# Sharing VectorE's shift passes with GpSimd, DMA transposes and a new fill rule in an interleaved attention kernel

## The chip, the cores and the metric

The kernel runs on one core of a Trainium2 chip. The metric is the device time of one execution in microseconds (us), lower is better. Each quoted time is the median of several executions of one kernel. A profile is one such execution, read by the hardware profiler.

## The reference, cut to what matters

Four blocks in a row work on 2048 rows of 512 numbers: attention block A, linear attention block B, then A and B again with the same weights. Nearly all of the time is in A: 32 heads share one key and value head of width 16, and each head needs a full 2048 x 2048 table of exponentials.

```python
def _A_ref(x, wq, wk, wv, wo):
    H = 32; Dh = D // H                          # D = 512, Dh = 16
    q = (x @ wq).reshape(B, S, H, Dh)            # S = 2048 (transposed to heads first)
    k = x @ wk                                   # one key head for all 32
    v = x @ wv
    scores = jnp.einsum("bhqd,bkd->bhqk", q, k) * (Dh ** -0.5)
    p = _softmax(scores, axis=-1)
    return jnp.einsum("bhqk,bkd->bhqd", p, v)... @ wo
# _B_ref: phi(t) = where(t > 0, t + 1, exp(t)) + 1e-6 of q and k, then linear attention
x = x + _A_ref(_layernorm(x), ...);  x = x + _B_ref(_layernorm(x), ...)
x = x + _A_ref(_layernorm(x), ...);  x = x + _B_ref(_layernorm(x), ...)
```

## The kernel before: the parts that matter

The program has no hand-written order. It describes operations with an estimated duration for each, and a small list scheduler runs them on a model clock while the program is being built. The engine of each operation and the order on each engine are then fixed, and semaphores hold the dependencies. An estimate in the program decides the order, but it is not a time on the chip.

The scores of the two A blocks fall into 2 x 2048 = 4096 tiles of 128 x 512. Each goes one of two ways:

- **ScalarE's way.** TensorE writes two or three score tiles into PSUM, ScalarE takes their exponential, and TensorE multiplies the result by the values (one pass per tile).
- **VectorE's way.** VectorE builds the bits of a bfloat16 exponential with integer arithmetic. A first pass reads the scores from PSUM. Three *shift passes* then add 32, 64 and 96 to the 16-bit words of four tiles at once, from SBUF to SBUF, and TensorE sums the four terms with weighted values (four value passes per tile).

```python
# one first pass per tile (PSUM -> SBUF)
o = add(DV, tdv(512), lambda e: e.tensor_scalar(out=PTD[:, hp.idx, 0, i * 512:(i + 1) * 512], in0=bank(db),
        scalar1=SCALE * LOG2E * 128.0, scalar2=TOFF, op0=ALU.mult, op1=ALU.add), ..., name="P1")
# after four of them: three shift passes per group, all on VectorE (SBUF -> SBUF)
for r in range(NTERM):                           # NTERM = 4
    dep = c["p1"]
    if r:
        dep = [add(DV, tdv(512 * m, 0.26), lambda e, r=r: e.tensor_scalar(out=PTD[:, hp.idx, r, 0:512 * m],
                   in0=PTD[:, hp.idx, 0, 0:512 * m], scalar1=float(SHIFT[r]), scalar2=None, op0=ALU.add),
                   deps=c["p1"], uses=[hp], prio=3.0, name="xo")]
    for i, p in enumerate(c["pos"]):
        pv = self.add_pv(p, PTD[:, hp.idx, r, i * 512:(i + 1) * 512].bitcast(BF16), hp, dep[0 if r else i], r, 1)
# ... cut: buffer release ...
# phi of block B: the exponential on ScalarE, then on GpSimd
o2 = add(PO, 0.65, lambda e: e.tensor_scalar(out=e_buf[:, he.idx, :], in0=e_buf[:, he.idx, :],
        scalar1=1.0, scalar2=1e-6, op0=ALU.min, op1=ALU.add), ..., name="phm")
# ... cut: VectorE combines max(scores, 0) with it; layer norm, transposes on TensorE, projections, ramp, tail
```

`DV` is VectorE, `PO` is GpSimd, `AC` is ScalarE. `idle()` (cut) adds filler matmuls where the model expects TensorE to be idle for long; they are meant to keep its granted clock up.

The softmax here doesn't subtract the row's maximum and nothing guards it: scores larger than these inputs give would overflow.

Of the kernel before, what the change touches and what calls it, by code (L numbers as in the profile page):

```python
# [14 lines left out]
LAT = {PE: 0.2, AC: 0.22, DV: 0.13, PO: 0.2, SP: 2.0}  # L15
STATS = {}
FLEX = 0.0
SWITCH, PASS = 0.1, 0.217
MP, AP, MF, AF = 1, 2.0, 0.4, 2.0

# [27 lines left out]
class Sched:  # L48
# [152 lines left out]
    def _start(self, e, o):  # L201
# [19 lines left out]
        o.vis = end + (3.0 if o.dma else LAT[e])  # L221
# [39 lines left out]
    def finalize(self):  # L261
# [20 lines left out]
        for e in self.engs:  # L282
            n = 0
            for o in self.order[e]:
                if o.dma:
                    o.val = 16
                elif o.marked:
                    n += 1
                    o.val = n
            STATS["sem_" + e] = n  # L290
# [6 lines left out]
    def emit(self, name, eng):  # L297
        for o in self.order[name]:
            best = {}
            for d in o.waits:  # L300
                key = ("dma", id(d)) if d.dma else d.eng
                if best.get(key, (None, -1))[1] < d.val:
                    best[key] = (d, d.val)
            for d, v in best.values():
                eng.wait_ge(self.dsems[id(d)] if d.dma else self.sems[d.eng], v)
            ins = o.fn(eng)
            if o.dma:
                ins.then_inc(self.dsems[id(o)], 16)
            elif o.marked:
                ins.then_inc(self.sems[name], 1)  # L310


class Banks:
# [7 lines left out]
    def slots(self, idx, kind):  # L321
        if kind == "set":
            return (3 * idx, 3 * idx + 1, 3 * idx + 2)
        if kind == "set2":
            return (3 * idx, 3 * idx + 1)
# [30 lines left out]
def bass_interleave_layers__grouped_kv_mqa__linear_attn_block__prompt_kernel(  # L356
# [17 lines left out]
    LEAD = 16  # L374
    KC = 2
    HOLD = 0.75
    PCONT = 1.5
    DB = (5, 6)
# [3 lines left out]
    AWIN, ATGT, ATGT2 = 1.7, 0.5, 0.6  # L382
# [32 lines left out]
    NPA, NPD = 5, 3  # L415
    PTA = sb("PTA", [P, NPA, 1536], BF16)
    PTD = sb("PTD", [P, NPD, NTERM, 2048], U16)
# [47 lines left out]
    def dma(fn, **kw):  # L465
        return add(SP, 0.08, fn, dma=True, **kw)

# [43 lines left out]
    def layer_norm(t, prio, cb, win=None):  # L511
# [5 lines left out]
        else:  # L517
            add(DV, 0.062, lambda e: e.tensor_scalar(out=veps[:, t:t + 1], in0=mv[:, t, 1:2], scalar1=1e-5, scalar2=None, op0=ALU.add),  # L518
                reads=[("mv", t)], writes=[("ve", t)], prio=prio - 0.02)
            add(PO, 0.5, lambda e: e.tensor_tensor(out=rstd[:, t:t + 1], in0=veps[:, t:t + 1], in1=mhalf[:, 0:1], op=ALU.pow),  # L520
                reads=[("ve", t), "mhalf"], writes=[("rs", t)], prio=prio)
        hx, hb = Holder(p_xn), H_()
        o = add(DV, tdv(512, 0.52), lambda e: e.tensor_scalar(out=xn_buf[:, hx.idx, :], in0=x_sb[:, t, :], scalar1=mv[:, t, 0:1],
                                                              scalar2=rstd[:, t:t + 1], op0=ALU.subtract, op1=ALU.mult),
                reads=[("x", t), ("mv", t), ("rs", t)], prio=prio - 0.03, acq=[hx], name="xn")

# [10 lines left out]
        o2 = add((DV, AC), {DV: 0.333, AC: tac(512)}, cp, deps=[o], uses=[hb], rel=[hb] + ([win] if win else []), writes=[("xnT", t)], prio=prio - 0.04, name="xnT", cb=cb)  # L537
# [51 lines left out]
    def q_proj(L, qb, g, prio):  # L589
# [7 lines left out]
        o2 = add((DV, AC), {DV: tdv(512), AC: tac(512)}, ev, deps=[o], uses=[h], rel=[h], writes=[("QT", qb % 2, g, t) for t in range(4)], prio=prio - 0.05, name="qev")  # L597
# [3 lines left out]
    def q_tile(L, t, prio):  # L601
# [14 lines left out]
        o2 = add((DV, AC), {DV: tdv(512), AC: tac(512)}, ev, deps=[o], uses=[h], rel=[h], writes=[("QT", 0, g, t) for g in range(NG)], prio=prio - 0.05, name="qev")  # L616
# [4 lines left out]
    class Ctl:  # L621
        def __init__(self):
# [4 lines left out]
            self.pd = 0  # L627
            self.taken = bytearray()
# [5 lines left out]
            self.tail = True  # L634

# [62 lines left out]
        def add_pv(self, p, src, hold, dep, r=0, wt=NTERM):  # L698
# [25 lines left out]
            def f(e):  # L724
                return e.matmul(ps[32 * c:32 * c + 32, 7 * 512:8 * 512], lhsT=Vaug[:, kt, r, :], rhs=src, start=opened[0], stop=opened[1],  # L725
# [36 lines left out]
        def step(self, now):  # L762
# [9 lines left out]
            if self.pa >= n:  # L772
                self.tail = True
                for b in DB:
                    self.dstep(b, set())
                return False
            for s in ((0,) if self.ramp else (0, 1)):
                if not (banks.free[3 * s] and banks.free[3 * s + 1]):
                    continue
                w = 3 - s  # L780
                if w == 3 and not banks.free[3 * s + 2]:
                    continue
# [11 lines left out]
                if HOLD < 3.0 and not self.ramp and not any(banks.free[b] for b in DB) and self.dcan():  # L794
# [4 lines left out]
                kind = "set" if w == 3 else "set2"  # L799
# [8 lines left out]
            if not self.ramp and sum(not o.done for o in self.p1s) < DMIN:  # L808
# [8 lines left out]
        def fill(self, s, got, kind):  # L817
# [15 lines left out]
            def f(e):  # L833
                if twice:
                    self.smm(e, got, 3 * s)
                return self.smm(e, got, 3 * s)
# [7 lines left out]
            oe = add(AC, tac(m * 512), lambda e: e.activation(PTA[:, hp.idx, 0:m * 512], bank(3 * s, m * 512), ACTF.Exp, scale=SCALE),  # L844
# [13 lines left out]
        def dstep(self, db, js):  # L858
# [6 lines left out]
            if not banks.free[db] or (db == 6 and self.waiting()):  # L865
                return False
            if self.dcur is None:
                if not p_ptd.free:
                    return False
                hp = Holder(p_ptd)  # L870
# [11 lines left out]
            if p >= n or not self.ok(p):  # L882
# [11 lines left out]
            o = add(DV, tdv(512), lambda e: e.tensor_scalar(out=PTD[:, hp.idx, 0, i * 512:(i + 1) * 512], in0=bank(db), scalar1=SCALE * LOG2E * 128.0,  # L894
# [9 lines left out]
        def dpass(self, c):  # L904
            hp = c["hp"]
            m = len(c["pos"])
            cnt = {"n": 0}
            for r in range(NTERM):
                dep = c["p1"]
                if r:  # L910
                    dep = [add(DV, tdv(512 * m, 0.26), lambda e, r=r: e.tensor_scalar(out=PTD[:, hp.idx, r, 0:512 * m], in0=PTD[:, hp.idx, 0, 0:512 * m], scalar1=float(SHIFT[r]),  # L911
                                                                                   scalar2=None, op0=ALU.add),
                               deps=c["p1"], uses=[hp], prio=3.0, name="xo")]
                for i, p in enumerate(c["pos"]):
                    pv = self.add_pv(p, PTD[:, hp.idx, r, i * 512:(i + 1) * 512].bitcast(BF16), hp, dep[0 if r else i], r, 1)
                    cb0 = pv.cb

                    def cb(o_, cb0=cb0):
                        cb0(o_)
                        cnt["n"] += 1  # L920
                        if cnt["n"] == m * NTERM:
                            sc.at(o_.vis, lambda: p_ptd.give(hp.idx, None))
                    pv.cb = cb

        def dcan(self):
            return not self.dhold() and (self.dcur is not None or bool(p_ptd.free))

        def dhold(self):
            return self.pa + LEAD + 4 >= len(self.pos)
# [3 lines left out]

    def activity(now):

        tot, first = 0.0, now
        for o in reversed(sc.order[PE]):
# [3 lines left out]
            if o.pk[0] == "P":  # L941
                b = min(b, first)
                first = min(first, o.t0)
            if b > a:
                tot += (b - a) * (RG / P * len(o.pk[1]) if o.pk[0] == "S" else 0.95)
        return tot / AWIN

    def idle(now):
# [20 lines left out]
        else:  # L969
            c = max(range(4), key=lambda c: sc.pgrp.get(c, 0.0) if sc.pk == "P" else 0.0)  # L970
            f = lambda e: e.matmul(ps[32 * c:32 * c + 32, 7 * 512:8 * 512], lhsT=zer[:, 0:32], rhs=maskx[:].bitcast(BF16)[:, 0:512],  # L971
                                   start=not owned, stop=True, skip_group_check=True)
            pk = ("P", (c,))
# [8 lines left out]
    def for_misc():  # L982
        if ctl.tail or (ctl.ramp and not (ctl.layer is not None and ctl.ok(0))):
            return (6, 5, 4, 3, 2, 1, 0)
        return (6, 5, 4, 3) if ctl.ramp else (6,)
# [4 lines left out]
    def epi_tr(L, qb, g, hos, fine):  # L990
        h = H_()
        pr = 4.0
        keys = [("OT", gg, g) for gg in range(NG)] if fine else [("OT", g, qs) for qs in range(4)]

# [10 lines left out]
        o2 = add((DV, AC), {DV: 0.333, AC: tac(512)}, cp, deps=[o], uses=[h], rel=[h], writes=keys, prio=pr, name="otc")  # L1005
# [6 lines left out]
    def epi_y(L, qb, qs):  # L1012
# [4 lines left out]
            deps=[o], uses=[h], rel=[h], writes=[("x", t)], prio=2.0, name="res", cb=lambda o_: b_prep(L, t))  # L1017


    def phi(h, o, dst, keys, prio, tiled=False):  # L1020
        he = Holder(p_e)
        o1 = add(AC, tac(512), lambda e: e.activation(e_buf[:, he.idx, :], bank(h.idx), ACTF.Exp), deps=[o], uses=[h], acq=[he], prio=0.5, name="phe")  # L1022
        o2 = add(PO, 0.65, lambda e: e.tensor_scalar(out=e_buf[:, he.idx, :], in0=e_buf[:, he.idx, :], scalar1=1.0, scalar2=1e-6, op0=ALU.min, op1=ALU.add),  # L1023
                 deps=[o1], uses=[he], prio=prio, name="phm")
        sh = (lambda a: a.rearrange("p (g n) -> p g n", g=NG)) if tiled else (lambda a: a)
        add(DV, tdv(512), lambda e: e.scalar_tensor_tensor(out=dst, in0=sh(bank(h.idx)), scalar=0.0, in1=sh(e_buf[:, he.idx, :]), op0=ALU.max, op1=ALU.add),  # L1026
            deps=[o2], uses=[h, he], rel=[h, he], writes=keys, prio=prio - 0.1, name="phf")

    def b_prep(L, t):
        def go(o_):  # L1030
# [11 lines left out]
            o2 = add((DV, AC), {DV: tdv(512), AC: tac(512)}, ev, deps=[o], uses=[h2], rel=[h2], writes=[("vB", t % NTK)], prio=2.1, name="vBe")  # L1042
# [5 lines left out]
            elif t % 4 == 3:  # L1048
                b = t // 4
                for g in range(NG):  # L1050
                    h = H_()
                    o = proj(h, [(wqkv_sb[:, ft, g * P:(g + 1) * P], xnT[:, ft, b * 512:(b + 1) * 512]) for ft in range(FT)], 512,
                             ["wqkv"] + [("xnT", tt) for tt in range(4 * b, 4 * b + 4)], pr + 0.2, name="pq")
                    phi(h, o, pqT[:, g, b * 512:(b + 1) * 512], [("pq", g, tt) for tt in range(4 * b, 4 * b + 4)], 2.4)
            if t == T - 1:
                b_main(L)
        layer_norm(t, 2.3, go)

# [13 lines left out]
    def kv_block(L, b):  # L1072
        tl = KVB[b]
        n, final = len(tl), b == len(KVB) - 1
        for hh in range(2):
            h = H_()
            o = None
            for i, t in enumerate(tl):
# [9 lines left out]
                o = add(PE, 0.172, f, reads=[(k, tt % NTK) for k in ("pk", "vB") for tt in rd], prio=3.4, name="kv", pk=ALL4, **kw)  # L1088
            dst = kvacc if b == 0 else kvtmp
            add(DV, tdv(KW), lambda e, hh=hh, h=h, dst=dst: e.tensor_tensor(out=dst[:, hh, :], in0=bank(h.idx, KW), in1=maskx[:], op=ALU.mult),  # L1090
                reads=["mask"], deps=[o], uses=[h], rel=[h], writes=[("kva" if b == 0 else "kvt", hh)], prio=1.9, name="kvm")
# [116 lines left out]
```

## Time and profile before

| | before |
|---|---|
| time at the outset, median of 3 | 1684.43 us (1681.29 to 1697.97) |
| ScalarE busy, all / score exponentials | 1530.4 / 1430.7 us |
| score tiles: ScalarE / VectorE | 3099 / 997 |
| VectorE busy | 1415.1 us (84%) |
| GpSimd busy | 170.5 us (10%) |
| mean granted TensorE clock | 0.973 |

The groups by shape of the kernel before. The columns are: line, engine, operation, output <- input, shapes, count | busy us, mean ns of one | idle us before, and what ended it. L844 is ScalarE's exponential, L894 VectorE's first pass, L911 its shift pass, L1023 GpSimd's min-then-add.

```profile
L844 ACT ACTIVATE PTA<-ps_all 128x1536 bf16<-128x1536 f32 x632 | 933.1, 1476 | 72.6 <-PE ps_all L688 68.9
...
L894 DVE TENSOR_SCALAR PTD<-ps_all 128x512 uint16<-128x512 f32 x997 | 676.3, 684 | 153.4 <-PE ps_all L688 149.0
L844 ACT ACTIVATE PTA<-ps_all 128x1024 bf16<-128x1024 f32 x601 | 632.6, 1053 | 17.1 <-PE ps_all L688 16.3
...
L911 DVE TENSOR_SCALAR PTD<-PTD 128x2048 uint16<-128x2048 uint16 x744 | 496.4, 685 | 5.0
...
L1023 POOL TENSOR_SCALAR e_buf<-e_buf 128x512 f32<-128x512 f32 x64 | 126.6, 1978 | 701.7 <-ACT e_buf L1022 686.0 <-ACT veps L515 7.8 <-ACT rstd L516 7.4
```

One ScalarE tile costs 1430.7 / 3099 = 0.46 us. A first pass or a shift pass takes about 685 ns as recorded; in the timeline consecutive ones start 0.60 us apart. Shift passes fill 499 us of VectorE.

Two of the table of 25 us windows (stretch, length, busy us of each engine with its instruction count, granted TensorE clock, DMA share, GB/s). In the first ScalarE is busy almost throughout, which is the rule in the steady stretches; in the second the clock has fallen and everything has slowed.

```profile
core 0: us, PE busy (x) PEld busy (x) DVE busy (x) ACT busy (x) POOL busy (x), PEclk, DMA share, GB/s
100.00:125.00 25.00, 23.84 (x233) 7.24 (x225) 22.03 (x41) 23.61 (x22) 3.25 (x2) 1.00 0.01 2
1000.00:1025.00 25.00, 24.34 (x151) 5.08 (x145) 15.18 (x26) 17.62 (x15) 0.00 (x0) 0.58 0.00 1
```

From the list of waits (who <- for whom: us in total, times, longest us):

```profile
DVE PTD L894 <- PE ps_all L688: 149.0, 248, 3.2
...
ACT PTA L844 <- PE ps_all L688: 85.3, 108, 7.4
...
DVE pqT L1026 <- POOL e_buf L1023: 35.5, 22, 6.5
DVE pk_tok L1026 <- POOL e_buf L1023: 25.4, 28, 1.5
```

ScalarE loses 85 us to late score matmuls. Last, a detail: a shift pass on VectorE that begins just after a GpSimd operation. These are the timelines of VectorE and of GpSimd (start us, us, engine, line, operation).

```profile
721.00 1.11 DVE L911 TENSOR_SCALAR PTD<-PTD 128x2048 uint16<-128x2048 uint16 x1
722.03 0.68 DVE L894 TENSOR_SCALAR PTD<-ps_all 128x512 uint16<-128x512 f32 x1
```
```profile
720.96 1.92 POOL L1023 TENSOR_SCALAR e_buf<-e_buf 128x512 f32<-128x512 f32 x1 [10.73 <-ACT e_buf L1022]
```

The shift pass started 0.04 us after GpSimd's min-then-add and took 1.11 us in place of 0.69, but it ended 0.77 us before GpSimd did.

### The profile page before, as it was taken

Reading aid. Unit: us, or ns where it says so; the run is one execution under the profiler, and the core shown is the slowest. Engines: PE = TensorE matmul, PEld = TensorE weight load, DVE = VectorE, ACT = ScalarE, POOL = GpSimd, SP = SyncE. Lnnn points to the kernel's source line nnn. Section 1 sums busy time; section 2 is a strip of 40 time slices with the busy share of each in tenths; the row PEclk is TensorE's granted clock in tenths of the full one; section 3 lists DMA queues with packets and bytes.
Section 4 is the critical chain, followed back from the end, with each engine's and each line's share of the span. In section 5 each row is a group of like instructions: output and inputs, shape, how many; then the busy total and the mean of one; then the engine's idle time right before and its main releaser. Section 6 shows DMA issues by size and latency. Waiting matters only on the chain.

```text
span 1694.3 us, 40968 instructions
## 1 busy us (share of the span) xinstructions
PE 1602.4 (95%) x18333; PEld 531.1 (31%) x18333; DVE 1415.1 (84%) x2525; ACT 1530.4 (90%) x1496; POOL 170.5 (10%) x157
## 2 busy tenths in 40 slices
PE   7999999999999799999899999999999999899998
PEld 4323223323333133332543222223332332232334
DVE  6898898889898588987788887788998888788875
ACT  6999999999999599998699988899999999899866
POOL 2000000010010101012210000001000100001032
PEclk9999999999999799999999988899999999999999
DMA  3000000000000000000000000000000000000001
GB/s 127 1 2 1 2 1 1 2 1 1 2 1 2 0 2 1 1 2 2 3 3 1 1 1 1 1 1 2 2 1 1 1 2 1 1 1 1 1 2 52
DMA packets 7776, 9.99 MB, mean 6 GB/s; under 512 B 1456, under 2 KB 7088, under 8 KB 7600
## 3 DMA queue, kind: packets, MB, share of 16 engines
q1 hardware_dynamic: 7600, 7.37, 1.3%
q8 instruction: 143, 2.34, 0.6%
q14 instruction: 33, 0.27, 0.1%
HBM read 5.28 MB, written 2.10 MB: 4 GB/s over the span
## 4 chain that ended last, share of the span: by engine, by line
PE 45%; ACT 34%; DVE 13%; POOL 6%; issue 2%; DMA 0%; SPq 0%; POOLq 0%; ACTq 0%
ACT PTA L844 32%; PE ps_all L688 18%; PE ps_all L725 17%; PE ps_all L459 6%; POOL e_buf L1023 6%; DVE PTD L894 4%; DVE PTD L911 3%; PE ps_all L746 2%; ACT e_buf L1022 1%; DVE pk_tok L1026 1%; DVE pqT L1026 1%; DVE Eo L737 1%; DVE stats L512 1%; PE ps_all L971 1%; PE ps_all L530 1%
## 5 line engine op out<-in xcount | busy, mean ns | idle before, releaser
L844 ACT ACTIVATE PTA<-ps_all 128x1536 bf16<-128x1536 f32 (+1 forms) x1234 | 1430.7, 1269 | 89.7 <-PE ps_all L688 85.3
L894 DVE TENSOR_SCALAR PTD<-ps_all 128x512 uint16<-128x512 f32 x997 | 676.3, 684 | 153.4 <-PE ps_all L688 149.0
L688 PE MATMUL ps_all<-QT,Kr 32*128 32x512 bf16 x4201 | 721.5, 388 | 21.7 <-DVE PTD L894 10.3
L725 PE MATMUL ps_all<-PTD,Vaug 128*32 128x512 bf16 x3988 | 586.4, 392 | 9.7 <-DVE Eo L737 7.6
L725 PE MATMUL ps_all<-PTA,Vaug 128*32 128x512 bf16 x3099 | 553.8, 393 | 0.5 <-ACT PTA L844 0.3
L911 DVE TENSOR_SCALAR PTD<-PTD 128x2048 uint16<-128x2048 uint16 (+1 forms) x750 | 499.3, 684 | 5.0
L688 PEld LDWEIGHTS ps_all<-QT,Kr 32*128 32x128 bf16 x4201 | 177.2, 91 | 528.0 <-ACT PTA L844 208.3
L725 PEld LDWEIGHTS ps_all<-PTD,Vaug 128*32 128x32 bf16 x3988 | 143.5, 95 | 198.8 <-issue 128.2
L725 PEld LDWEIGHTS ps_all<-PTA,Vaug 128*32 128x32 bf16 x3099 | 132.2, 94 | 208.6 <-issue 182.5
L1023 POOL TENSOR_SCALAR e_buf<-e_buf 128x512 f32<-128x512 f32 x64 | 126.6, 1978 | 701.7 <-ACT e_buf L1022 686.0
L520 POOL TENSOR_TENSOR rstd<-veps,mhalf 128x1 f32<-128x1 f32 x26 | 23.2, 894 | 739.6 <-DVE veps L518 685.8
L459 PE MATMUL ps_all<-wqkv_sb,xnT 128*32 128x512 bf16 x1024 | 81.6, 386 | 8.5 <-DVE pk_tok L1026 7.1
L1022 ACT ACTIVATE e_buf<-ps_all 128x512 f32<-128x512 f32 x64 | 39.2, 612 | 19.7 <-PE ps_all L459 19.3
L746 PE MATMUL ps_all<-identf,Eo 128*128 128x128 f32 x256 | 44.7, 300 | 11.9 <-DVE pk_tok L1026 8.4
L459 PE MATMUL ps_all<-xnT,wqkv_sb 128*32 128x128 bf16 (+1 forms) x896 | 41.3, 300 | 11.7 <-DVE pqT L1026 10.9
L1026 DVE SCALAR_TENSOR_TENSOR pqT<-ps_all,e_buf 128x512 bf16<-128x512 f32 x32 | 21.9, 689 | 35.6 <-POOL e_buf L1023 35.5
L459 PE MATMUL ps_all<-xnT,wq_sb 128*32 128x128 bf16 (+1 forms) x896 | 44.8, 301 | 3.5 <-issue 3.4
L512 DVE BATCH_NORM_STATS2 stats<-x_sb 128x6 f32<-128x512 bf16 x64 | 42.8, 676 | 2.8 <-DMA x_sb<-in_A_x_dram 2.7
L737 DVE COPY Eo<-ps_all 128x512 f32<-128x512 f32 x63 | 42.9, 681 | 1.9 <-PE ps_all L746 1.2
L1026 DVE SCALAR_TENSOR_TENSOR pk_tok<-ps_all,e_buf 128x512 bf16<-128x512 f32 x32 | 22.1, 691 | 25.5 <-POOL e_buf L1023 25.4
L459 PE MATMUL ps_all<-wo_sb,OT 128*32 128x512 bf16 x512 | 41.2, 382 | 0.3 <-DVE pqT L1026 0.2
L746 PEld LDWEIGHTS ps_all<-identf,Eo 128*128 128x128 f32 x256 | 28.6, 148 | 32.2 <-DVE pk_tok L1026 12.7
(82 smaller groups left out, 707.8 us busy)
## 6 DMA issues: line engine op xcount, KB each, us to landing
out_dram<-x_sb SPq DMA_DIRECT2D x16, 128.0 KB, 1.7
x_sb<-in_A_x_dram SPq DMA_DIRECT2D x3, 512.0 KB, 6.7
wqkv_sb<-in_B_wqkv_dram SPq DMA_DIRECT2D x1, 1536.0 KB, 12.1
x_sb<-in_A_x_dram SPq DMA_DIRECT2D x2, 256.0 KB, 3.1
wq_sb<-in_A_wq_dram SPq DMA_DIRECT2D x1, 512.0 KB, 4.9
wo_sb<-in_A_wo_dram SPq DMA_DIRECT2D x1, 512.0 KB, 8.5
wo_sb<-in_B_wo_dram SPq DMA_DIRECT2D x1, 512.0 KB, 11.5
wk_sb<-in_A_wk_dram SPq DMA_DIRECT2D x1, 16.0 KB, 2.5
```

The lines of the kernel that those rows point to most:

```text
L459: i = e.matmul(out[32 * c:32 * c + 32], lhsT=lhsT[:, 32 * c:32 * c + 32], rhs=rhs, start=start, stop=stop, skip_group_check=True)
L512: add(DV, tdv(512), lambda e: e.bn_stats(stats[:, t, 0:6], x_sb[:, t, :]), reads=[("x", t)], writes=[("st", t)], prio=prio, name="bn")
L688: x = e.matmul(bank(b0 + k), lhsT=Kr[r, m, kt * P:(kt + 1) * P], rhs=QT[r, self.units[u][0] % 2, gs, q0:q0 + n], start=True, stop=True)
L725: return e.matmul(ps[32 * c:32 * c + 32, 7 * 512:8 * 512], lhsT=Vaug[:, kt, r, :], rhs=src, start=opened[0], stop=opened[1], skip_group_ch ...
L737: return (e.copy if oe.eng == AC else e.tensor_copy)(Eo[:, he.idx, :], bank(7))
L746: i = e.transpose(bank(ht.idx, P, qs * P), Eo[:, he.idx, qs * P:(qs + 1) * P], identf[:])
L844: oe = add(AC, tac(m * 512), lambda e: e.activation(PTA[:, hp.idx, 0:m * 512], bank(3 * s, m * 512), ACTF.Exp, scale=SCALE), deps=[o] + pr ...
L894: o = add(DV, tdv(512), lambda e: e.tensor_scalar(out=PTD[:, hp.idx, 0, i * 512:(i + 1) * 512], in0=bank(db), scalar1=SCALE * LOG2E * 128. ...
L911: dep = [add(DV, tdv(512 * m, 0.26), lambda e, r=r: e.tensor_scalar(out=PTD[:, hp.idx, r, 0:512 * m], in0=PTD[:, hp.idx, 0, 0:512 * m], sc ...
L1022: o1 = add(AC, tac(512), lambda e: e.activation(e_buf[:, he.idx, :], bank(h.idx), ACTF.Exp), deps=[o], uses=[h], acq=[he], prio=0.5, name= ...
L1023: o2 = add(PO, 0.65, lambda e: e.tensor_scalar(out=e_buf[:, he.idx, :], in0=e_buf[:, he.idx, :], scalar1=1.0, scalar2=1e-6, op0=ALU.min, o ...
L1026: add(DV, tdv(512), lambda e: e.scalar_tensor_tensor(out=dst, in0=sh(bank(h.idx)), scalar=0.0, in1=sh(e_buf[:, he.idx, :]), op0=ALU.max, o ...
```

## The change

The intent is to free VectorE, so that it takes more of the 4096 tiles from ScalarE. A shift pass may now run on GpSimd or VectorE, whichever the scheduler finds free. Each term gets its own 4 KB buffer (12 of them, in place of 3 buffers of 16 KB). Layer norm and attention output are transposed by DMA in the steady stretch. VectorE's score fills wait when ScalarE is about to finish (`LX`). GpSimd takes over phi's sum. Several estimates, priorities and the filler rule are set anew.

```diff
-    LEAD = 16
+    LEAD, LEAD2 = 28, 12
-    AWIN, ATGT, ATGT2 = 1.7, 0.5, 0.6
+    AWIN, ATGT, ATGT2 = 2.8, 0.42, 0.42
-    NPA, NPD = 5, 3
+    NPA, NPD, NT0 = 5, 12, 5
-    PTD = sb("PTD", [P, NPD, NTERM, 2048], U16)
+    PTD = sb("PTD", [P, NPD, 2048], U16)
+        def shift(self, c, m, r, done):
+            hp, ht = c["hp"], Holder(p_ptd)
+
+            def f(e):
+                kw = dict(scalar2=1.0, op1=ALU.mult) if o.eng == PO else dict(scalar2=None)
+                return e.tensor_scalar(out=PTD[:, ht.idx, 0:512 * m], in0=PTD[:, hp.idx, 0:512 * m], scalar1=float(SHIFT[r]), op0=ALU.add, **kw)
+            o = add((PO, DV), {PO: PXO[0] + 512 * m * PXO[1], DV: tdv(512 * m, 0.26)}, f, deps=c["p1"], uses=[hp], acq=[ht], prio=3.0, cb=done, name="xo")
+            return [o], ht
 ... steady transposes (the same for the attention output):
+        if late:
+            tdma(lambda e: [e.dma_start(xnT[:, ft, t * P:(t + 1) * P], xn_buf[:, hx.idx, ft * P:(ft + 1) * P], transpose=True) for ft in range(FT)], ...
 ... the fill rule:
-            if not self.ramp and sum(not o.done for o in self.p1s) < DMIN:
+            if not self.ramp and sum(not o.done for o in self.p1s) < DMIN and not (LX0 < sc.tfree[AC] + LAT[AC] - now < LX and not all(banks.free[a] for a, w in SETS)):
 ... phi: GpSimd's min-then-add becomes min-then-max, and GpSimd also adds the two halves
-        o2 = add(PO, 0.65, ... scalar1=1.0, scalar2=1e-6, op0=ALU.min, op1=ALU.add), ...
+        o3 = add(PO, PHM, ... scalar1=1.0, scalar2=0.0, op0=ALU.min, op1=ALU.max), ...
 ... cut: the late search for tiles (LEAD2), estimates, priorities, filler matmuls, which banks serve what
```

## The prediction

> **What bounds it.** The table of 25 us windows shows two long steady stretches (about 50 to 800 and 870 to 1640 us) in which ScalarE is busy 23.5 to 25 of 25 us. ScalarE sets the pace there: by the groups by shape, 1234 exponentials, 1430.7 us, covering 3099 of 4096 score tiles (512 columns each), 0.46 us of ScalarE per tile. VectorE does the other 997. Its tiles cost a first pass (684 ns recorded, but consecutive ones start 0.60 us apart in the timeline) and three quarters of a 128x2048 shift pass (685 ns, also 0.60 apart): 1.06 us. VectorE is 84% busy and idles 149 us waiting for its scores. Matmul's 95% busy rests on modelled ends, so I do not read it as the limit. GpSimd is 10% busy. The granted clock dips (0.58 to 0.87) in about seven windows; ScalarE loses roughly 39 us there (estimate, against normal windows).
>
> **What changes.**
> 1. A shift pass may run on GpSimd. GpSimd's copy of 128x512 took 616 ns, so I estimate 2.4 us for 2048; but its min-then-add on 128x512 took 1922 ns, which would mean 7.7 us. The added multiply by 1.0 suggests a form known to run fast; I take 2.5 us.
> 2. About 80 DVE copies of 0.41 us after transposes (about 25 us busy) become DMA transposes, whose latency nothing in the steady stretch waits for.
> 3. The phi sum moves to GpSimd (32+32 times), replaced on VectorE by a pass of the same length: even.
> 4. VectorE's score fills yield to ScalarE's: aimed at the 85 us that the waits list puts between score matmuls and ScalarE.
> 5. New fillers and activity count: maybe fewer clock dips.
>
> **Costed.** With ScalarE's steady time T = 0.4617 x (4096 - D) + 95 us, VectorE 80% filled (0.604 D + 0.604 x shifts left + 137 us of other work), and GpSimd 75 to 80% filled at 2.5 us, the balance is D about 1200, GpSimd about 420 of 900 shifts, T about 1433 against about 1550 now: 117 us saved.
>
> Against it: the Trainium skill, "SBUF — State Buffer", section "Who interferes with whom", says that a VectorE op in a 2-port mode and a GpSimd op exclude each other for a whole instruction. The trace agrees in part: shift passes that start within 0.45 us of a GpSimd start are stretched to as much as 1108 ns, and GpSimd's 1.92 becomes up to 2.42; later starts are not held. A GpSimd shift reads four times as many elements, so I expect about 0.4 us more per remaining VectorE shift: with that the balance gives about 1497, a saving of only 53 us. I take the middle (85 us), plus 25 us from fewer clock dips and fills. Ramps and tails stay.
>
> **Predicted: 1575 us, range 1490 to 1660. Faster by over 2%: 0.85; within 2%: 0.08; slower: 0.07.**
>
> **What shows it.** Right: VectorE first passes near 1150 to 1250, ScalarE exponentials under 1370 us busy, GpSimd 60 to 85% busy with some 350 to 500 shifts of 2.2 to 2.8 us, VectorE shifts lengthened (mean over 0.75 us), fewer windows with a granted clock under 0.9. Wrong: GpSimd shifts of 5 us or more and TensorE's weight loads waiting for GpSimd in the hundreds of us; or first passes near 1000.
>
> **What would make it wrong.** A slow GpSimd form (far slower than now); much longer holds (near 1650); TensorE as the true limit, as each VectorE tile takes four value passes against one; or holds absorbed (about 1520).

## The result, and the profile after

| | before | changed |
|---|---|---|
| median, 4 runs each | 1687.56 us | **1934.68 us** (1917.16 to 1956.4) |
| ratio of the fast runs | 1 | **1.143** (95% interval 1.135 to 1.151) |
| first passes on VectorE | 997 | 1150 |
| shift passes VectorE / GpSimd | 750 / 0 | 526 / 338 |
| mean VectorE shift pass, 128x2048 | 685 ns | 1233 ns |

The changed kernel is 14% slower. Ratios in this document divide the mean time of one kernel's fast runs by that of the other's of the same rounds, so they are not quite the ratio of the medians quoted. The profiled execution of the changed kernel (1956.4 us, clock 0.896) fell in the slow state; its three fast runs had 1917 to 1938 us at a clock of 0.909 to 0.925. So I check its main reading below on a fast run of almost the same kernel (e13).

The groups by shape of the changed kernel, with columns as before. L861 is ScalarE's exponential, L918 the first pass, L960 the shift pass on either engine.

```profile
L861 ACT ACTIVATE PTA<-ps_all 128x1536 bf16<-128x1536 f32 x610 | 887.6, 1455 | 329.1 <-PE ps_all L704 324.1
...
L918 DVE TENSOR_SCALAR PTD<-ps_all 128x512 uint16<-128x512 f32 x1150 | 763.5, 681 | 205.1 <-PE ps_all L704 201.8
L960 POOL TENSOR_SCALAR PTD<-PTD 128x2048 uint16<-128x2048 uint16 x338 | 727.2, 2156 | 792.7 <-DVE PTD L918 711.5 <-PE ps_all L741 46.9 <-DVE veps L526 19.1
L960 DVE TENSOR_SCALAR PTD<-PTD 128x2048 uint16<-128x2048 uint16 x523 | 639.7, 1233 | 9.5 <-PE ps_all L741 4.2
...
L861 ACT ACTIVATE PTA<-ps_all 128x1024 bf16<-128x1024 f32 x558 | 573.4, 1028 | 76.5 <-PE ps_all L704 73.7
```

ScalarE's exponentials got less work, as intended, but its idle time just before them rose to 329.1 + 76.5 us. First passes, which read PSUM, are as long as before (681 ns). Shift passes on VectorE became 1233 - 685 = 548 ns longer each. GpSimd's own shifts are fast (2.16 us).

The timelines of the changed kernel at one such place, VectorE first, then GpSimd, then TensorE's weight loads:

```profile
176.41 0.69 DVE L918 TENSOR_SCALAR PTD<-ps_all 128x512 uint16<-128x512 f32 x1 [1.39 <-PE ps_all L704]
177.14 2.99 DVE L960 TENSOR_SCALAR PTD<-PTD 128x2048 uint16<-128x2048 uint16 x2
180.05 0.67 DVE L918 TENSOR_SCALAR PTD<-ps_all 128x512 uint16<-128x512 f32 x1
```
```profile
177.18 2.40 POOL L960 TENSOR_SCALAR PTD<-PTD 128x2048 uint16<-128x2048 uint16 x1 [4.70 <-DVE PTD L918]
```
```profile
178.77 0.09 PEld L704 LDWEIGHTS ps_all<-QT,Kr 32*128 32x128 bf16 x2 [0.42 <-issue]
180.18 0.10 PEld L741 LDWEIGHTS ps_all<-PTD,Vaug 128*32 128x32 bf16 x2 [1.32 <-DVE PTD L960]
```

The last first pass made all three shifts of the group ready at the same moment. VectorE took one, and GpSimd started 0.04 us later. VectorE's two shifts then took 2.99 us in place of 1.28; e6 below shows that a VectorE shift is held until GpSimd's is nearly over. TensorE's fixed order had the values of that term next, so its weight loads stood still for 1.32 us, and behind them ScalarE's next scores. The list of waits has this in sum:

```profile
POOL PTD L960 <- DVE PTD L918: 711.5, 224, 8.9
ACT PTA L861 <- PE ps_all L704: 397.8, 405, 5.3
...
DVE PTD L918 <- PE ps_all L704: 201.8, 287, 3.5
...
PEld ps_all L741 <- DVE PTD L960: 81.6, 105, 1.8
...
PE ps_all L741 <- DVE PTD L960: 43.6, 64, 1.3
```

ScalarE's wait for scores grew from 85 to 398 us. GpSimd itself waits 711 us for the next group, so it is no bottleneck. Two windows, as before: even at full clock ScalarE is busy 19.5 us of 25 in place of 23.6, and there are many more windows with a low clock (25 of the first 66 have less than 0.9 in this slow run, against 7 before).

```profile
100.00:125.00 25.00, 22.89 (x213) 6.46 (x210) 24.18 (x37) 19.51 (x17) 13.81 (x7) 1.00 0.03 7
400.00:425.00 25.00, 25.00 (x143) 4.92 (x141) 16.61 (x23) 14.29 (x13) 6.19 (x3) 0.52 0.03 6
```

### The profile page after: what moved, and what is told of

Its sections match the earlier page's. It is cut to its first block, busy times and chain, and to the rows that moved or that the text cites. A ratio compares the mean times of both kernels' runs of the same rounds, so it can differ in the third digit from the quotient of the medians.

```text
span 1954.7 us, 42449 instructions
## 1 busy us (share of the span) xinstructions
PE 1755.4 (90%) x18794; PEld 523.5 (27%) x18794; DVE 1655.2 (85%) x2402; ACT 1492.6 (76%) x1418; POOL 901.6 (46%) x563
## 4 chain that ended last, share of the span: by engine, by line
DVE 53%; PE 44%; ACT 1%; issue 1%; DMA 0%; POOL 0%; SPq 0%; POOLq 0%; ACTq 0%
DVE PTD L960 25%; DVE PTD L918 20%; PE ps_all L704 17%; PE ps_all L741 17%; PE ps_all L464 8%; PE ps_all L762 2%; DVE Eo L753 1%; DVE xn_buf L532 1%; DVE stats L520 1%; DVE e_buf L1068 1%; ACT PTA L861 1%; DVE x_sb L1061 1%; DVE Osb L772 1%; DVE v_tok L1088 0%; DVE QT L610 0%
## 5 line engine op out<-in xcount | busy, mean ns | idle before, releaser
L861 ACT ACTIVATE PTA<-ps_all 128x1536 bf16<-128x1536 f32 (+1 forms) x1168 | 1397.5, 1251 | 405.6 <-PE ps_all L704 397.8
L960 POOL TENSOR_SCALAR PTD<-PTD 128x2048 uint16<-128x2048 uint16 x338 | 727.2, 2156 | 792.7 <-DVE PTD L918 711.5
L918 DVE TENSOR_SCALAR PTD<-ps_all 128x512 uint16<-128x512 f32 x1150 | 763.5, 681 | 205.1 <-PE ps_all L704 201.8
L704 PE MATMUL ps_all<-QT,Kr 32*128 32x512 bf16 x4199 | 772.3, 417 | 101.7 <-DVE PTD L918 86.0
L741 PE MATMUL ps_all<-PTD,Vaug 128*32 128x512 bf16 x4600 | 622.9, 429 | 53.1 <-DVE PTD L960 43.6
L960 DVE TENSOR_SCALAR PTD<-PTD 128x2048 uint16<-128x2048 uint16 x526 | 641.2, 1229 | 9.5 <-PE ps_all L741 4.2
L1070 POOL TENSOR_SCALAR e_buf<-e_buf 128x512 f32<-128x512 f32 x64 | 48.1, 751 | 90.7 <-ACT e_buf L1067 90.5
L1073 POOL TENSOR_TENSOR pk_tok<-e_buf 128x512 bf16<-128x512 f32 x32 | 41.9, 1310 | 21.5 <-DVE e_buf L1068 21.2
L1073 POOL TENSOR_TENSOR pqT<-e_buf 128x512 bf16<-128x512 f32 x32 | 43.4, 1357 | 17.8 <-DVE e_buf L1068 17.0
L1068 DVE TENSOR_SCALAR e_buf<-ps_all 128x512 f32<-128x512 f32 x64 | 43.5, 680 | 9.4 <-ACT e_buf L1067 9.3
```

The source lines that it names most:

```text
L704: x = e.matmul(bank(b0 + k), lhsT=Kr[r, m, kt * P:(kt + 1) * P], rhs=QT[r, self.units[u][0] % 2, gs, q0:q0 + n], start=True, stop=True)
L741: return e.matmul(ps[32 * c:32 * c + 32, 7 * 512:8 * 512], lhsT=Vaug[:, kt, r, :], rhs=src() if callable(src) else src, start=opened[0], s ...
L861: oe = add(AC, tac(m * 512), lambda e: e.activation(PTA[:, hp.idx, 0:m * 512], bank(SETS[s][0], m * 512), ACTF.Exp, scale=SCALE), deps=[o] ...
L960: return e.tensor_scalar(out=PTD[:, ht.idx, 0:512 * m], in0=PTD[:, hp.idx, 0:512 * m], scalar1=float(SHIFT[r]), op0=ALU.add, **kw)
L1068: o2 = add(DV, tdv(512), lambda e: e.tensor_scalar(out=e_buf[:, hr.idx, :], in0=bank(h.idx), scalar1=0.0, scalar2=1e-6, op0=ALU.max, op1=A ...
L1070: o3 = add(PO, PHM, lambda e: e.tensor_scalar(out=e_buf[:, he.idx, :], in0=e_buf[:, he.idx, :], scalar1=1.0, scalar2=0.0, op0=ALU.min, op1 ...
```

## The experiments

**Theory P (the port hold).** While GpSimd runs a shift pass, a VectorE pass from SBUF to SBUF is held. The two engines' shifts become ready together, so they collide all the time, and the fixed order hands the delay to TensorE and ScalarE.

**Rivals.** (R1) The rest of the change: DMA transposes, fill rule, larger lead, fillers, four value passes per additional VectorE tile. (R2) A busy GpSimd as such: late minima and powers on which others wait. (R3) TensorE's falling clock as the cause and not the companion.

In all runs with a changed description the scheduler makes a new order. In e3, e4, e7 and e8 the order of TensorE, VectorE and ScalarE is that of the kernel before, instruction for instruction (compared in the built programs). All kernels gave correct results. Every profile quoted below is of a fast run.

### e1: all shift passes on VectorE, the rest of the change kept

```diff
-            o = add((PO, DV), {PO: PXO[0] + 512 * m * PXO[1], DV: tdv(512 * m, 0.26)}, f, deps=...
+            o = add(DV, tdv(512 * m, 0.26), f, deps=...
```

> The changed kernel with every shift pass on VectorE; the DMA transposes, fill rule, bigger lead, fillers and small buffers all stay (the program orders its instructions anew). Port theory (the loss comes from VectorE's shift passes being held while GpSimd shifts): VectorE's shift passes return from 1229 to about 685 ns and the time to about the kernel before, 1690 us (1640 to 1720). Rival (the loss comes from the rest of the change: fill rule, DMA transposes, fillers, TensorE's order and its clock): it stays above 1800 us.

Measured: 1679.42 us, ratio to before 0.995 (0.989 to 1.001). The shift passes are back at a mean of 708 ns:

```profile
L960 DVE TENSOR_SCALAR PTD<-PTD 128x2048 uint16<-128x2048 uint16 x828 | 573.3, 708 | 3.7 <-PE ps_all L741 1.0
```

So the rest of the change does not lose the 14% by itself: R1 falls. It gains almost nothing either. VectorE takes 1108 tiles here and ScalarE's exponentials are shorter, but ScalarE's wait for scores rises from 85 to 132 us.

### e2: all shift passes on GpSimd

```diff
+            o = add(PO, PXO[0] + 512 * m * PXO[1], f, deps=...
```

> The changed kernel with every shift pass on GpSimd, so VectorE has no shift pass to be held. Port theory: GpSimd shifts stay near 2.16 us, GpSimd over 80% busy in the steady stretch limits VectorE to some 700 to 900 tiles, and the time is 1640 to 1740 us, well under the changed kernel's 1930. Rival (rest of the change): above 1800 us.

Measured: 2551.02 us, ratio 1.510. By the numbers the rival (above 1800 us) was met and the port theory missed. But the time has another reason, which I had not foreseen, so this run does not separate the theories. The groups by shape show why:

```profile
L960 POOL TENSOR_SCALAR PTD<-PTD 128x2048 uint16<-128x2048 uint16 x1128 | 2107.7, 1915 | 18.7 <-PE ps_all L741 11.9 <-DVE PTD L918 6.6
L918 DVE TENSOR_SCALAR PTD<-ps_all 128x512 uint16<-128x512 f32 x1508 | 990.5, 689 | 864.1 <-PE ps_all L704 857.0
```

The scheduler gave VectorE 1508 tiles although GpSimd could not follow: 1134 shifts at 1.9 us are 2.1 ms by themselves. Two readings are still of use. A GpSimd shift without VectorE shifts beside it takes 1.915 us, not 2.16, so in the changed kernel GpSimd is held too. And the first passes stay at 689 ns beside a GpSimd that is 89% busy, so passes that read PSUM are not held.

### e3 and e4: the kernel before with work on GpSimd that nobody needs

After every group of four first passes of the kernel before, one or two GpSimd operations are inserted (332 in all) which read a constant weight tensor and write a tensor that is unused in that stretch (`Msb`). The e3 load is the shift form; the e4 load is the min-then-add of the kernel before, nearly as long but with a quarter of the elements.

```diff
+# after sc.run(): walk the finished order; o is the last first pass of a group
+new.append(extra(lambda e: e.tensor_scalar(out=Msb (2048 x uint16), in0=wqkv_sb (2048 x uint16),
+           scalar1=32.0, scalar2=1.0, op0=ALU.add, op1=ALU.mult), deps=[o, ...]))          # e3
+new.append(extra(lambda e: e.tensor_scalar(out=Msb (512 x float32), in0=wqkv_sb (512 x float32),
+           scalar1=1.0, scalar2=1e-6, op0=ALU.min, op1=ALU.add), deps=[o, ...]))           # e4
```

> The kernel before, with the order of TensorE, VectorE and ScalarE kept instruction for instruction, plus 332 GpSimd shift passes (128x2048 uint16, one or two at the end of each group of four first passes) whose result nobody uses. Port theory: VectorE's shift passes are stretched from 685 ns to 1000 ns or more, and the time grows by 150 us or more, to 1840 us or above. Rival: nothing waits for this load but 64 minima and 26 powers on GpSimd, so within 3% of before (under 1735 us).

> Control for the run with the shift load: the same 332 places, but each GpSimd operation is the min-then-add on 128x512 float32, which was about as long (1.92 us) in the kernel before and held VectorE only in its first 0.45 us. Port theory: VectorE's shift passes stay under 850 ns in the mean and the time is 1690 to 1760 us, far below the run with the shift load. If a busy GpSimd as such (late minima and powers, semaphores) were the cause, both loads would cost the same.

Measured: e3 2187.12 us, ratio 1.296 (1.288 to 1.304); e4 1870.79 us, ratio 1.110 (1.100 to 1.120). The groups by shape, first e3, then e4 (L911 is VectorE's shift, L1192 the load):

```profile
L911 DVE TENSOR_SCALAR PTD<-PTD 128x2048 uint16<-128x2048 uint16 x744 | 787.5, 1076 | 5.0
L1192 POOL TENSOR_SCALAR Msb<-wqkv_sb 128x2048 uint16<-128x2048 uint16 x332 | 725.1, 2184 | 1096.9 <-DVE PTD L894 1068.5 <-DVE veps L518 15.6 <-DVE mv L513 5.1
```
```profile
L1192 POOL TENSOR_SCALAR Msb<-wqkv_sb 128x512 f32<-128x512 f32 x332 | 750.3, 2260 | 761.4 <-DVE PTD L894 737.6 <-DVE veps L518 11.1 <-DVE mv L513 4.4
...
L911 DVE TENSOR_SCALAR PTD<-PTD 128x2048 uint16<-128x2048 uint16 x744 | 545.6, 751 | 5.0
```

GpSimd's busy time in the load is the same (725 and 750 us), but VectorE's shifts become 1076 ns with the one and 751 ns with the other. The order of the other engines is that of before, and no result of the load is used, so the 316 us between e3 and e4 go with the hold and not with GpSimd's busy time. But e4 was a miss: I expected at most 1760. Its shifts lost only (751 - 685) x 744 = 49 us, so the larger part of its 181 us must come by another way (at the dearest price of a hold measured below, 1.6 us for each us, the 49 us explain about 80). VectorE waits for GpSimd's minima for 61 us in the kernel before, and for 110 us here (plus 14 us for powers). That is R2: it seems to exist beside the hold, and the next pair tests it.

### e7 and e8: the same loads where no minimum or power is near

```diff
-            if n1 % 4 == 0:                       # one or two operations per group
+            if n1 % 4 == 0 and not any(-9.0 < t - o.t0 < 9.0 for t in busy):   # busy: minima and powers; one per group
```

> The kernel before with its order kept and idle-result GpSimd shift passes as in the run with the shift load, but only one per group and only where the schedule has no minimum or power within 9 us, so that lateness of those cannot count. Port theory: VectorE's shifts are stretched wherever they meet the load, and the time still grows by 80 us or more. If the lateness of minima and powers caused most of the 495 us of the fuller load, it is within 3% of before.

> The short min-then-add load in the same cleared places. Port theory: the hold is only its first 0.45 us, VectorE's shifts mean under 760 ns, time within 3% of before (up to 1740 us); then most of the 180 us of the fuller short load was lateness of minima and powers, not the port.

Measured, with 100 loads left in each: e7 1840.56 us, ratio 1.090 (1.083 to 1.097); e8 1699.62 us, ratio 1.007 (0.999 to 1.014). The groups by shape, e7 and then e8:

```profile
L911 DVE TENSOR_SCALAR PTD<-PTD 128x2048 uint16<-128x2048 uint16 x744 | 595.0, 817 | 5.0
...
L1193 POOL TENSOR_SCALAR Msb<-wqkv_sb 128x2048 uint16<-128x2048 uint16 x100 | 221.5, 2215 | 641.2 <-DVE PTD L894 641.2
```
```profile
L911 DVE TENSOR_SCALAR PTD<-PTD 128x2048 uint16<-128x2048 uint16 x744 | 513.4, 707 | 5.0
L1193 POOL TENSOR_SCALAR Msb<-wqkv_sb 128x512 f32<-128x512 f32 x100 | 234.8, 2348 | 532.9 <-DVE PTD L894 532.9
```

Lateness is out of the way: VectorE waits 60 us for GpSimd's minima in e7 and 61 us in e8, as in the kernel before. A hundred operations of nearly equal length then cost 155 us in one form and about 14 us, not clear of zero, in the other. The traces show it shift by shift: of the separately listed VectorE shifts, those that began 1.0 to 1.2 us after the start of a load took 1.71 us in the mean in e7 (18 of them) and 0.68 us in e8 (22). This settles P against R2 for this load, and it leaves lateness as the likely reason of the larger part of e4's 181 us. It also gives the price: the holds sum to (817 - 685) x 744 = 98 us, and the time grows by 155 us. One microsecond of hold cost 1.6 us here.

The pair also answers half of R3. The order is fixed and only the load differs, yet the granted clock was 0.922 to 0.931 in e7, against 0.971 to 0.983 in e8 and 0.971 to 0.986 in the kernel before of the same rounds. So here the clock falls because of the holds and is not the first cause. How much of the 155 us its fall adds is not separated; the 1.6 contains it.

One expectation was too simple. The short load does not hold VectorE only in its first 0.45 us. In e8, 20 of the 35 separately listed shifts that began 1.3 us or more after its start, and before its end, took 0.76 to 1.10 us. The holds stay small (707 ns in the mean).

### e5 and e6: two shifts on VectorE, one on GpSimd, in order and without order

Both kernels give GpSimd exactly the third shift of each group. In e5 VectorE's two come right after the last first pass and GpSimd's waits for both, so it runs beside VectorE's next four first passes. In e6 all three become ready together.

```diff
+            if r < NTERM - 1:
+                o = add(DV, tdv(512 * m, 0.26), f, deps=c["p1"], ..., prio=0.9, ...)     # e6: prio=3.0
+                c.setdefault("xd", []).append(o)
+            else:
+                o = add(PO, PXO[0] + 512 * m * PXO[1], f, deps=c["p1"] + c["xd"], ...)   # e6: deps=c["p1"]
```

> The changed kernel, but each group's shift passes have fixed places: two on VectorE right after the group's last first pass, then the third on GpSimd, which waits for both, so that it runs beside VectorE's next four first passes (which read PSUM). Port theory: VectorE's shift passes are under 800 ns in the mean, and VectorE is rid of a third of them without being held: faster than the kernel before, 1590 to 1680 us. Rival (GpSimd sharing costs time however it is ordered, or TensorE is the limit): no better than 1700 us.

> The same split (two shifts on VectorE, one on GpSimd) without the order: all three become ready together, as in the changed kernel. Port theory: VectorE's shifts are held again, above 950 ns in the mean, and the time is 1780 us or more. If only the amount of work on GpSimd mattered, it would equal the interleaved run within 2%.

Measured on the same chip: e5 **1664.22 us**, ratio 0.986 (0.980 to 0.992); e6 1920.97 us, ratio 1.140 (1.131 to 1.149). The shift passes in the groups by shape, e5 and then e6:

```profile
L960 POOL TENSOR_SCALAR PTD<-PTD 128x2048 uint16<-128x2048 uint16 x278 | 527.8, 1899 | 733.0 <-DVE PTD L960 655.4 <-PE ps_all L741 75.8 <-PE ps_all L704 1.7
L960 DVE TENSOR_SCALAR PTD<-PTD 128x2048 uint16<-128x2048 uint16 x556 | 388.2, 734 | 6.6 <-PE ps_all L741 2.0
```
```profile
L960 DVE TENSOR_SCALAR PTD<-PTD 128x2048 uint16<-128x2048 uint16 x568 | 653.0, 1158 | 6.4 <-PE ps_all L741 1.5
L960 POOL TENSOR_SCALAR PTD<-PTD 128x2048 uint16<-128x2048 uint16 x284 | 619.3, 2181 | 860.7 <-DVE PTD L918 797.1 <-PE ps_all L741 31.7 <-DVE veps L526 24.5
```

The work on GpSimd is the same (278 and 284 shifts of full width), only its place differs. The holds differ by (1158 - 734) x 568 = 241 us, the times by 257 us, and e6 is as slow as the changed kernel. ScalarE's waits, e5 and then e6:

```profile
ACT PTA L861 <- PE ps_all L704: 128.8, 120, 6.0
```
```profile
ACT PTA L861 <- PE ps_all L704: 356.4, 361, 5.4
```

The two descriptions differ in one dependence and one priority, but the scheduler then orders everything anew, and the clock differs too (0.983 and 0.916 in the profiles). So this pair alone does not exclude that e6's order is worse for another reason; e7, whose order is fixed, shows that holds cost time without a new order.

In e6 I sorted VectorE's separately listed shifts by how long after the latest separately listed GpSimd shift they began. Those that began about 0.5 us after it took 2.00 us in the mean (52 of them), about 1.25 us after it 1.71 us (41), about 1.75 us after it 1.14 us (44), and those that began after its end 0.71 us. Start plus stretch (the length less 0.69) gives 1.8 to 2.3 us: VectorE is held until the GpSimd shift is nearly over.

### e9: only the ordered third, taken into the kernel before

```diff
 # in the kernel before, with its 16 KB buffers:
+                    if r < NTERM - 1: dep = [add(DV, ..., deps=c["p1"], prio=0.9, name="xo")]; c.setdefault("xd", []).append(dep[0])
+                    else:             dep = [add(PO, 0.1 + 512 * m * 1.1e-3, ..., deps=c["p1"] + c["xd"], prio=3.0, name="xo")]
```

> Only the ordered share taken into the kernel before: of each group's three shift passes two stay on VectorE right after the last first pass, the third runs on GpSimd after them; nothing else of the change. Port theory: VectorE's shifts keep a mean under 760 ns and the time is 1640 to 1680 us, faster than before by 0.5 to 2.5%. If the rest of the change (DMA transposes, fill rule, larger lead, small buffers) is what lets VectorE take more tiles, this gains nothing and stays within 0.5% of before.

Measured: 1691.08 us, ratio 1.004 (1.002 to 1.007). Its shifts are 692 ns in the mean, so hardly anything is held, yet it gains nothing (it is 0.4% slower): the port theory's 1640 to 1680 us was a miss, and the other alternative was met. VectorE takes only 1012 tiles, and its first passes sit idle for 239 us waiting for scores (149 us before). Freed VectorE time is not used here. Which part of the change makes it usable is shown only in part, by e11. One candidate was not tested: e9 keeps the old min-then-add, for which VectorE waits 64 us, while e5 lists no such wait.

### e10: more filler matmuls in the changed kernel

```diff
-    AWIN, ATGT, ATGT2 = 2.8, 0.42, 0.42
+    AWIN, ATGT, ATGT2 = 2.8, 0.75, 0.42          # 1051 fillers planned in place of 345
```

> The changed kernel with about three times as many filler matmuls (1051 against 345) from a higher activity target. If TensorE's lowered granted clock multiplies the loss (holds leave TensorE idle, its clock falls, everything waits longer), the granted clock rises above 0.95 and the time falls by 30 to 90 us, to 1840 to 1900; VectorE's shifts stay held at about 1.2 us. If the clock is only a companion, the time stays within 1.5% of 1930.

Measured: 1938.5 us, ratio 1.149, clock 0.917 to 0.935. The fillers hardly lifted the clock (0.909 to 0.925 in the changed kernel's fast runs), so this run says nothing for or against R3. A likely reason, not tested: fillers are placed where the scheduler expects idle time, and the holds are what it does not expect. How much of the loss comes through the clock stays open. An estimate: in e13's steady windows with a clock of at least 0.99, I count about 61 tiles in 25 us (ScalarE's exponential time divided by 0.4617 us, plus first passes), and about 57 in the others. The kernel before has about 68 in its full-clock windows. So by this count most of the loss is there at full clock as well.

### e11 and e12: parts of the change around the interleaved order

```diff
 # e11, on e5: steady transposes back on TensorE
-        late = not (ctl.ramp or ctl.tail)
+        late = False                              # and the same for the attention output
 # e12, on e5: no fill rule
-LX0, LX = 0.0, 0.5
+LX0, LX = 0.0, 0.0
```

> The interleaved kernel with the steady transposes back on TensorE and their copies on VectorE. If the DMA transposes are worth what VectorE's saved copies (some 25 us busy) suggest, it is 0.3 to 1.5% slower than the interleaved run's 1664 us: 1670 to 1690 us.

> The interleaved kernel without the rule that VectorE's score fills wait when ScalarE is about to finish. If the rule helps, ScalarE's wait for score matmuls rises from 129 us and the time by 0.5% or more (1672 us or above); if it is a trade of one wait for the other, within 0.5% of 1664 us.

Measured: e11 1668.75 us, ratio 0.991 (0.989 to 0.993); e12 **1649.57 us**, ratio 0.980 (0.978 to 0.981). Against e5 (0.986, 0.980 to 0.992, from other rounds) neither is clearly apart. The two differ from one another, but in two things. Without the DMA transposes VectorE takes 1042 tiles in place of 1116. e12 answers the other way from what the rule is meant to do: ScalarE's wait for scores is 117 us without it and 129 us with it. e12 has the lowest time, 2.0% below the kernel before.

### e13, e14 and e15: what the rule and the third on GpSimd are worth

e13 is the changed kernel without the fill rule. e14 is e12 with GpSimd's shift entered at its measured time. e15 is e1 without the fill rule.

```diff
-LX0, LX = 0.0, 0.5
+LX0, LX = 0.0, 0.0                               # all three
-POW, PXO = 1.0, (0.1, 1.1e-3)
+POW, PXO = 1.0, (0.05, 0.9e-3)                   # e14 only: 1.89 us in place of 2.35
```

> The changed kernel with only the fill rule taken out. If the hold alone makes the loss, it stays at 1880 us or more, with VectorE's shifts still above 1.1 us; if the rule was a large part of the loss, it falls below 1850.

> The interleaved kernel without the fill rule, and with GpSimd's shift entered in the schedule at its measured 1.90 us in place of 2.35. If the estimate costs anything, 1635 to 1645 us; otherwise within 0.5% of 1650.

> All shifts on VectorE and no fill rule. If GpSimd's ordered third is worth something, this is slower than the interleaved one without the rule (1650): 1662 to 1690 us. If the gain of that run came from dropping the rule alone, it equals it within 0.5%.

Measured: e13 1926.23 us, ratio 1.143 (1.138 to 1.148); e14 1654.19 us, ratio 0.982 (0.979 to 0.985); e15 1738.17 us, ratio 1.033 (1.029 to 1.037). The fill rule has no part in the loss of the changed kernel, and the wrong estimate of GpSimd's shift costs nothing in e14. The profile of e13, a fast run, has nearly the same VectorE shifts as the slow page above (1222 and 1233 ns):

```profile
L960 DVE TENSOR_SCALAR PTD<-PTD 128x2048 uint16<-128x2048 uint16 x520 | 632.0, 1222 | 7.8 <-PE ps_all L741 2.6
```

And GpSimd's ordered third is worth something: e14, on the same chip, is 5% faster than e15, which has every shift on VectorE (0.982 against 1.033). e15 is slower than I had expected at most (1690 us). In e15 VectorE takes 1174 tiles (1123 in e14) and ScalarE waits 210 us for scores (118 in e14). With the rule on, the same comparison (e1 at 0.995, e5 at 0.986, from different rounds) is small. My reading, not tested further: the rule hides a VectorE that is too full, and it is of no use once VectorE has room.

## Why the prediction was wrong

It said 1575 us, 1490 to 1660, with 0.85 for faster. The chip said 1935.

- **What bounds the kernel** was read well enough for the kernel before: ScalarE is nearly always busy in the steady stretch. But "Matmul's 95% busy rests on modelled ends, so I do not read it as the limit" left out that every engine is fed through TensorE's fixed order. Wherever VectorE took more tiles, most of ScalarE's saved time came back as its wait for scores: 51 us less of exponentials and 47 us more wait in e1, 52 and 44 us in e5.
- **GpSimd's shift** was taken at 2.5 us. It is 1.90 us alone and 2.16 us among VectorE's shifts. The feared 7.7 us did not come. Right.
- **The tiles**: "D about 1200, GpSimd about 420 of 900 shifts". Measured 1150, and 338 of 864. The tiles were nearly right; GpSimd got less than forecast (46% busy in place of 60 to 85%).
- **The step that failed** is the price of the collision: "I expect about 0.4 us more per remaining VectorE shift: with that the balance gives about 1497, a saving of only 53 us", and then "I take the middle (85 us)". The mechanism was named, but its term was mis-sized. The hold was 0.55 us per shift, 548 ns x 523 = 287 us. The larger error is that I charged it to VectorE's capacity, as if the work could be shared out anew. With a fixed order it is charged to the time: 241 us of hold cost 257 us between e5 and e6, and 98 us of hold cost 155 us in e7. A term worked out as 64 us (1497 against 1433), and halved to 32 us by taking the middle, was worth about 250: the changed kernel is 255 us slower than e1, which has no shift on GpSimd.
- **Why the holds were so frequent** was missed: the prediction does not ask how often the two engines meet. In this program the three shifts of a group become ready at the same instant, so the engines that share them meet again and again.
- **"plus 25 us from fewer clock dips and fills"** had the wrong sign. TensorE's idle time rose and its granted clock fell from 0.973 in the profile before to between 0.909 and 0.925 in the fast runs. How much of the loss goes through the clock is not settled (e10).
- **"holds absorbed (about 1520)"**: with the holds taken away by ordering, the program ran at 1650 to 1664. The 117 us of the balance never existed in full. What limits the use of the freed VectorE time is not shown; e9's first passes waited 239 us for scores.

## What to carry to other kernels

Before giving part of an engine's work to a second engine, ask what the two share, and put the shared operations where they cannot meet: the same split cost 14% when the passes became ready together (e6) and gained 1.4% when one waited for the other (e5). The gain is not sure, as e9 shows. In a program whose order is fixed at build time, charge a hold to the time at about its full length (1.1 and 1.6 us for each us here), not to the engine's average load. To test a suspected contention, add the suspected operation with an unused result to the unchanged order, beside a control of equal length.

## What the Trainium skill lacked or had wrong

- "SBUF — State Buffer", section "Who interferes with whom", says that a VectorE op in a 2-port mode and a GpSimd op exclude each other for the whole instruction. This holds nearly for GpSimd's shift of 2048 uint16 (VectorE held until about 1.8 to 2.3 us after its start, worked out from e6's stretches). It does not hold for GpSimd's min-then-add on 512 float32: that took 1.92 us or more, VectorE shifts that started with it were stretched to at most 1.11 us, and those that started 1.0 to 1.2 us after it were not held (0.68 us, 22 of them in e8), although some that started later were (0.76 to 1.10 us). With equal GpSimd busy time the mean VectorE shift was 1076 ns beside the one and 751 ns beside the other (e3, e4). No run shows in which mode VectorE's shift runs. The same section says that a VectorE instruction with at most one SBUF input, outside the 2-port modes, does not contend with GpSimd. The runs agree: first passes, which read PSUM, took 689 ns beside a GpSimd that was 89% busy (e2).
- "GPSIMD Engine Reference", section "Engine selection", calls one-input GpSimd operations roughly line-rate. The pair of operations in one instruction matters, and no page says so: on 128x512 float32 min-then-add took 1.92 us, and min-then-max 631 ns in the mean (e5). Add-then-multiply on 128x2048 uint16 took 1.90 us.
- "VectorE: DVE Perf Modes", section "The three transpose paths", gives 1309 ns for a 128x128 bfloat16 transpose by DMA. Here the median from issue to landing was 2.3 to 2.4 us, in the changed kernel. The ends measured may not be the same.
- No page says what a hold costs in a program with a fixed order: 1.1 us of time for each us of hold between e5 and e6, 1.6 us in e7.
